# First k stack issued two groups sooner in the key stage, V's maxima begun a group later, the loop's first score moved behind a V group

## The chip, the cores and the metric

The kernel runs on one core of one Trainium2 chip. The metric is the device time of one execution in microseconds (us). Before the change the median of three runs is 1766.57 us (1765.93 to 1769.04).

## The reference

Two attention blocks work on inputs of their own, 2048 positions by 640 columns with 32 heads of 20, and their outputs are joined side by side. Block A attends to a window of 8 positions at a distance of 2. Block B, in which the change lies, is full softmax attention:

```python
qkv = (x @ wqkv).reshape(B, S, 3, H, Dh).transpose(2, 0, 3, 1, 4)
q, k, v = qkv[0], qkv[1], qkv[2]
scores = jnp.einsum("bhqd,bhkd->bhqk", q, k) * (Dh ** -0.5)
p = _softmax(scores, axis=-1)
o = jnp.einsum("bhqk,bhkd->bhqd", p, v)
return o.transpose(0, 2, 1, 3).reshape(B, S, D) @ wo
```

## The kernel before, in words

Each fp32 operand of a projection is split into a high part (an fp32r copy) and a low part (the difference), and three matmuls take the place of one: high by high, high by low, low by high (`PASSES`). PE is TensorE, DVE is VectorE, ACT is ScalarE, POOL is GpSimd; SP is the engine on which nearly all DMAs are issued. Every engine keeps the order in which the code is written.

The stages run one after the other. First the q, k and v of block A are projected. Then come k and q of block B: five pairs of weight tiles (`m` from 0 to 8), each with four blocks of 512 positions (`n`) and two tiles (`j`). A tile is 15 matmuls on PE; ACT casts the result (`pr`), DVE takes the difference, and SP stores both, 512 KB, to `qb_d` or `kb_d` in DRAM. In the last pair, `m == 8`, loads for what follows stand between these stores:

- `wide_pieces(wv_b[0])`, three pieces of the first half of V's weights, into `stg`; ACT casts each into `ww` (high), DVE subtracts (low). In (n, j) = (3, 0) the three pieces of the second half are issued at once, and their casts stand on ACT behind the copy of the second V group.
- `b_keys(0)`, the first group's k stack `bk`: four loads from `kb_d`, of 40, 22, 40 and 22 rows of 16 KB (640 and 352 KB), one each behind the tiles of n = 2 and n = 3.
- `b_queries(0, qc)`, the q rows `bq`: four loads for each of four blocks `qc`, issued behind V's groups.

Then V of block B is projected in 32 groups (`v_group`, L958): 15 matmuls into one bank of PSUM, a copy by ACT into one of four `ve` tiles, a store by SP to `vb_d`. The groups take the position blocks 2, 3, 0, 1, and in each first the four groups of the first weight half, then four of the second. So the fifth group is the first that needs the second half. The last two groups (`v_late`) belong to the loop. From the seventh group on a step of maxima, `b_max` (L753), follows each group: four matmuls of q by k for 128 queries and 1024 keys in two heads, into two pairs of banks (banks 4 to 7, `wide`), and one DVE reduction of each pair. All 24 steps (`LEAD`) must be through before the loop.

The loop (`b_units`, L883) is written out by hand as lists of tokens. `P` adds one step of exponentials by V (the first two `P` are V's two late groups), `ss` is two scores, `MM` two maxima, `sm` one of each, `G` and `V` are work of block A. Each token takes its banks by a planner's clocks (`one`, `two`, L143). The first unit of 16 steps uses `UNIT_V`, as do those that follow it. It begins:

```python
    UNIT_V = (
        "sm P sm MM ss P sm ss MM sm P ss MM sm P sm sm MM sm V sm ss MM sm P sm MM ss P sm MM sm ss P sm MM "
```

Of the kernel before, what the change touches and what calls it, by code (L numbers as in the profile page):

```python
# [40 lines left out]
NKB = 16  # L41
UP = 12
NS = NG * NQC * NKB
LEAD = 24
# [21 lines left out]
def attention_pair(ctx, tc, xa, wqk_a, wv_a, wo_a, xb, wqk_b, wv_b, wo_b, oa, ob):  # L66
# [13 lines left out]
    def after(n, fn, *args):  # L80
        due.setdefault(now[0] + n, []).append((fn, args))
# [22 lines left out]
    def tick():  # L104
        now[0] += 1
        for fn, args in due.pop(now[0], ()):
            fn(*args)
# [81 lines left out]
    def big(home, shape, name):  # L189

        return sb.tile(shape, F32R, tag=f"big{home}", bufs=1, name=name)
# [6 lines left out]
    def chunk(t, xi, k):  # L198
        return t[k // (KC - 1)][:, xi, k % (KC - 1)]

    def x_pieces(x, n, second=None, at=()):

        t = columns(*at or (n,))
        src = x[:, n * 512:(n + 1) * 512].rearrange("(k p) c -> p k c", p=128)

        def piece(a, b):
            u = t[a // (KC - 1)]
            m = a % (KC - 1)
            split(u[:, 0, m:m + b - a], u[:, 1, m:m + b - a], src[:, a:b], "p", second)
        return t, [lambda a=a, b=b: piece(a, b) for a, b in PAIRS]  # L210
# [55 lines left out]
    def m_pieces(m):  # L266
        w = sb.tile([128, 2, KC, 128], F32R, tag="w", bufs=4, name="w")
        return w, [lambda: split(w[:, 0], w[:, 1], wqk_b[m])]
# [35 lines left out]
    NT = S // 128  # L304
# [11 lines left out]
    t, more = x_pieces(xa, 1, at=(2,))  # L316
# [5 lines left out]
    t, loads = x_pieces(xa, 2, at=(3,))  # L322
# [263 lines left out]
    def b_keys(g):  # L586
        k = big(3 * (g % 2), [128, 2, S], "bk")
        v = sb.tile([128, NKB, VG], F32, tag="vb", bufs=2, name="vb")
        stacks[g] = (k, v)
        return [lambda r=r, r0=r0, s0=s0, n=n: sp.dma_start(  # L590
            k[r * HALF + r0:r * HALF + r0 + n].bitcast(F32), kb_d[s0:s0 + n, g * GH + 2 * r:g * GH + 2 * r + 2])
            for r in range(2) for r0, s0, n in BK_RUNS]
# [14 lines left out]
    def dst_b(m, n):  # L607
        def rows(d):
            return d[:2 * DH].rearrange("(t d) h s -> t (d h) s", t=2)[:, (m % KC) * 128:(m % KC + 1) * 128]
        return rows(qb_d[n]) if m < KC else rows(kb_d)[:, :, n * 512:(n + 1) * 512]  # L610

    groups = 0
    for m in range(0, 10, 2):
        nxt = []
        for n in range(4):
            for j in range(2):
                p = next(banks)
                for k in range(KC):
                    for i, (wi, xi) in enumerate(PASSES):
                        pe.matmul(p, WB[j][:, wi, k], chunk(XB[n], xi, k), start=(k == 0 and i == 0),  # L620
                                  stop=(k == KC - 1 and i == 2))
                c = MS[m + j]
                o = (0, 1) if c < KC else (1, 0)
                pt = sb.tile([128, 2, 512], F32R, tag="p", bufs=PB, name="pr")
                act.copy(pt[:, o[0]], p)
                dve.tensor_tensor(pt[:, o[1]], p, pt[:, o[0]].bitcast(F32), ALU.subtract)
                after(1, sp.dma_start, dst_b(c, n).rearrange("t p c -> p t c"), pt.bitcast(F32))
                tick()
                if loads:
                    loads.pop(0)()  # L630
                if m < 8 and (n, j) in ((1, 0), (1, 1)):
                    w, loads = m_pieces(MS[m + 2 + len(nxt)])
                    nxt.append(w)
                elif m == 8 and (n, j) == (0, 1):
                    WV, loads = wide_pieces(wv_b[0])
                elif m == 8 and n == 3:
                    if j == 0:
                        wait[0] = 4
                        w1, more = wide_pieces(wv_b[1])
                        for fn in more:  # L640
                            fn()
                if m == 8 and n > 1:
                    if (n, j) == (2, 0):
                        k_loads = b_keys(0)
                        rings.append(big(1, [128, NQC, 2, 512], "bq"))
                        q_loads = [fn for qc in range(NQC) for fn in b_queries(0, qc)]
                    k_loads.pop(0)()
                groups += 1
                if 4 < groups < 34 and groups * 2 % 5 < 2:
                    next(a_work, None)  # L650
        WB = nxt
# [112 lines left out]
    P = {}  # L764
# [71 lines left out]
    def b_two(what):  # L836
# [35 lines left out]
    PAIR = "P ss MM sm P sm ss MM sm sm".split()  # L872
    UNIT = (
        "P ss MM sm P sm ss MM sm sm P ss MM sm P sm MM ss sm sm P sm MM ss P sm MM ss sm sm P ss MM sm P "
        "sm MM ss sm sm P ss MM sm P sm ss MM ss G sm ss MM sm P sm MM ss P sm MM sm ss P sm MM ss P sm "
        "MM sm ss P MM MM ss P ss MM sm sm").split()
    UNIT_V = (
        "sm P sm MM ss P sm ss MM sm P ss MM sm P sm sm MM sm V sm ss MM sm P sm MM ss P sm MM sm ss P sm MM "
        "ss P sm MM sm ss P sm sm sm P sm ss MM ss G sm MM ss sm P sm MM ss P sm MM sm ss P sm sm sm P sm ss "
        "MM sm P sm MM ss P sm MM ss").split()  # L880
    SLOT = UNIT[:UNIT.index("G")].count("P") - 1

    def b_units(pv, group, more):  # L883

        scores = ((i, pl, r) for i in range(NS - LEAD) for pl in range(2) for r in range(2))
        maxima = ((m, j) for m in range(LEAD, NS) for j in range(2))
        steps = iter(range(-LAG, NS))
        half = []
        for i in range(0, NS - LEAD, NKB):
            for t in UNIT_V if i // NKB < 6 * (NT - UP) else UNIT if i + NKB <= NS - LEAD else PAIR * (NKB // 4):  # L890
                if t == "P":
                    yield
                    pv(next(steps))
                elif t == "G":
                    group()
                elif t == "V":
                    more()
                elif t == "ss":
                    b_two([("s", *next(scores)) for _ in range(2)])
                elif t == "MM":  # L900
                    m, j = next(maxima)
                    max_tiles(m)
                    b_two([("m", m, j, r) for r in range(2)])
                    max_end(m, 1)
                else:
                    s = next(scores)
                    shut = bool(half)
                    m, j, r = half.pop() if shut else (*next(maxima), 1 - s[2])
                    max_tiles(m)
                    if not shut:  # L910
                        half.append((m, j, 1 - r))
                    b_two([("s", *s), ("m", m, j, r)])
                    if shut:
                        max_end(m, 1)
# [39 lines left out]
    steps = iter(range(LEAD))  # L954
    WV = [WV, w1]
    groups = 0
# [66 lines left out]
    for n, half, s in V_GROUPS[:-LAG]:  # L1023
        v_group(n, half, s)
        tick()
        groups += 1
        if q_loads:
            for _ in range(4 if groups == 1 else 1):
                q_loads.pop(0)()
        if groups == 1:  # L1030
            wait[0] = 5
        if groups in (8, 16):
            XB[groups // 8 - 1], more = x_pieces(xb, groups // 8 - 1, gp, (groups // 8 - 1, groups // 8 + 1))
            for fn in more:
                fn()
        if groups > 6:
            for i in islice(steps, 1):
                b_max(i)
        if groups in (9, 11, 15, 17, 19, 23, 25, 28):
            next(a_work, None)  # L1040
        if groups in (22, 23, 26):
            v_piece(0, *((8, 12), (12, 16), (0, 4))[(groups - 21) // 2])
        if groups in (18, 21):
            a_columns(UP + groups // 21)
        if groups == 24:
            for n, fn in enumerate(a_load()):
                after(2 + n, fn)
        if groups == 14:
            a_turn(*done_a.pop(0)[1:])
        turn_parts()  # L1050
        if groups == 28:
            wait[0] = 2
            load_out(wo_a, WO, (0,))
        if loads and groups >= 28:
            loads.pop(0)()
# [33 lines left out]
    steps = b_units(lambda i: b_pv(i) if i >= 0 else v_group(*v_late.pop(0)), group, a_more)  # L1089
    next(steps)  # L1090
    for i in range(NS + LAG):
# [12 lines left out]
        if i > 14 and i % 4 == 3 and next(a_work, 0) == 0:  # L1104
            for d in done_a:
                d[0] -= 1
        if i % NKB == SLOT and done_a and done_a[0][0] <= 0:
            beside.append((lambda d=done_a.pop(0): a_turn(*d[1:]),))
# [76 lines left out]
```

## Time and profile before

| | |
|---|---|
| median of the runs | 1766.57 us (1765.93 to 1769.04) |
| the profiled execution | 1765.34 us |
| its span in the trace | 1763.5 us |
| PE busy | 1749.7 us (99%) |
| DVE / ACT / POOL busy | 1346.4 / 1333.1 / 1229.7 us |
| share of the chain that ended last: PE, DVE | 88%, 6% |
| granted PE clock | 1.00 |
| DMA over the span | 152 GB/s |

The profiled execution's own time is its span and 1.84 us around it. A row of the timeline gives the start in us from the span's start, the time that the row's instructions take together, the engine, the operation with its tiles (written from read), and how many instructions the row joins; in square brackets stands how long the engine was idle before, and what released it. Tiles of PSUM are all called `ps_st`. `ww,xn` and `ww,xl` are a V group, `bk,bq` (read by PE as q by k) a maximum, `bq,bk` a score, `e,vb` a `P`. SPq is SP's queue, in which the issue of a DMA takes some 0.4 us and can wait like any instruction.

### The profile page before, as it was taken

Reading aid. Unit: us, or ns where it says so; the run is one execution under the profiler, and the core shown is the slowest. Engines: PE = TensorE matmul, PEld = TensorE weight load, DVE = VectorE, ACT = ScalarE, POOL = GpSimd, SP = SyncE. Lnnn points to the kernel's source line nnn. Section 1 sums busy time; section 2 is a strip of 40 time slices with the busy share of each in tenths; the row PEclk is TensorE's granted clock in tenths of the full one; section 3 lists DMA queues with packets and bytes.
Section 4 is the critical chain, followed back from the end, with each engine's and each line's share of the span. In section 5 each row is a group of like instructions: output and inputs, shape, how many; then the busy total and the mean of one; then the engine's idle time right before and its main releaser. Section 6 shows DMA issues by size and latency. Waiting matters only on the chain.

```text
span 1763.5 us, 31971 instructions
## 1 busy us (share of the span) xinstructions
PE 1749.7 (99%) x11331; PEld 998.7 (57%) x11331; DVE 1346.4 (76%) x1821; ACT 1333.1 (76%) x2598; POOL 1229.7 (70%) x1086
## 2 busy tenths in 40 slices
PE   9999999999999999999999999999999999999999
PEld 7988888874454444444444444444444444444569
DVE  3102333679999999999999999999999999999400
ACT  4323222229989999999999999989999999989981
POOL 0000683595888888888989888988888888745442
PEclk9999999999999999999999999999999999999999
DMA  7657868774536554644474456536552635222123
GB/s 260 194 172 241 301 240 268 239 233 118 158 100 172 142 163 127 152 134 135 154 172 138 133 150 157 160 100 177 140 159 91 144 109 143 62 73 63 57 72 114
DMA packets 212152, 269.74 MB, mean 153 GB/s; under 512 B 91676, under 2 KB 131740, under 8 KB 211000
## 3 DMA queue, kind: packets, MB, share of 16 engines
q1 hardware_dynamic: 211416, 267.04, 50.5%
q8 instruction: 89, 1.46, 0.3%
q10 hardware_dynamic: 576, 0.66, 0.1%
q14 instruction: 71, 0.58, 0.1%
HBM read 192.87 MB, written 74.74 MB: 152 GB/s over the span
## 4 chain that ended last, share of the span: by engine, by line
PE 88%; DVE 6%; POOL 2%; DMA 1%; issue 1%; ACT 1%; SPq 0%; DVEq 0%; POOLq 0%; ACTq 0%
PE ps_st L61 88%; DVE mx L61 6%; POOL akv L61 1%; DMA bk<-kb_d 1%; ACT e L61 1%; POOL xn L61 0%; DMA vb_d<-ve 0%; SPq L61 0%; POOL ww L61 0%; POOL braw L61 0%; DMA stg<-xa 0%; POOL ao L61 0%; DMA rb<-s_d 0%; POOL xl L61 0%; POOL aot L61 0%
## 5 line engine op out<-in xcount | busy, mean ns | idle before, releaser
L61 DVE TENSOR_REDUCE mx<-ps_st 128x1 f32<-128x512 f32 (+1 forms) x1500 | 1219.3, 879 | 76.0 <-PE ps_st L61 66.2
L61 ACT ACTIVATE e<-ps_st 128x512 f32<-128x512 f32 x2048 | 1067.3, 608 | 36.3 <-PE ps_st L61 17.8
L61 PE MATMUL ps_st<-bq,bk 62*128 62x512 f32 x2048 | 610.3, 440 | 0.8 <-DVE mx L61 0.6
L61 PEld LDWEIGHTS ps_st<-bq,bk 62*128 62x128 f32 x2048 | 288.4, 184 | 479.0 <-ACT e L61 351.9
L61 PE MATMUL ps_st<-bk,bq 60*128 60x512 f32 x2048 | 555.4, 433 | 2.6 <-DVE mx L61 1.8
L61 PE MATMUL ps_st<-e,vb 128*32 128x512 f32 x4096 | 542.9, 604 | 3.2
L61 POOL TENSOR_TENSOR braw<-braw,more 128x512 f32<-128x512 f32 x224 | 287.9, 1285 | 147.3 <-ACT more L61 137.2
L61 POOL TENSOR_TENSOR akv<-akv,aq 128x1280 f32<-128x1280 f32 x64 | 188.5, 2946 | 184.7 <-DMA akv<-ka_d 184.7
L61 POOL TENSOR_TENSOR akv<-akv 128x640 f32<-128x640 f32 (+3 forms) x304 | 282.7, 930 | 23.8
L61 PEld LDWEIGHTS ps_st<-bk,bq 60*128 60x128 f32 x2048 | 269.4, 184 | 34.0 <-DVE mx L61 12.5
L61 ACT COPY ro<-ps_st 128x320 f32<-128x320 f32 (+2 forms) x132 | 62.6, 476 | 192.2 <-PE ps_st L61 160.0
L61 PEld LDWEIGHTS ps_st<-e,vb 128*32 128x32 f32 x4096 | 82.0, 108 | 158.9 <-issue 72.4
L61 POOL TENSOR_TENSOR akv<-akv,al 128x1280 f32<-128x1280 f32 x64 | 151.9, 2374 | 0.2
L61 ACT COPY more<-ps_st 128x512 f32<-128x512 f32 x224 | 132.5, 592 | 1.6 <-PE ps_st L61 1.4
L61 PE MATMUL ps_st<-ww,xn 128*128 128x320 f32 x768 | 125.8, 314 | 0.0
L61 PEld LDWEIGHTS ps_st<-ww,xn 128*128 128x128 f32 x768 | 113.6, 188 | 19.7 <-ACT e L61 8.4
L61 PE MATMUL ps_st<-xn,w 128*128 128x512 f32 x480 | 117.6, 393 | 0.0
L61 PEld LDWEIGHTS ps_st<-xn,w 128*128 128x128 f32 x480 | 90.1, 188 | 21.0
L61 ACT CAST pr<-ps_st 128x512 fp32r<-128x512 f32 x40 | 23.6, 589 | 103.5 <-PE ps_st L61 103.5
L61 PE MATMUL ps_st<-wc,xn 128*128 128x512 f32 (+1 forms) x432 | 101.5, 380 | 0.1
L61 DVE TENSOR_TENSOR pr<-ps_st,pr 128x512 fp32r<-128x512 f32 x40 | 27.7, 692 | 93.0 <-ACT pr L61 90.2
L61 PEld LDWEIGHTS ps_st<-wc,xn 128*128 128x128 f32 x432 | 80.3, 189 | 14.2 <-ACT xn L61 0.5
(71 smaller groups left out, 1065.7 us busy)
## 6 DMA issues: line engine op xcount, KB each, us to landing
akv<-ka_d SPq DMA_DIRECT2D x128, 320.0 KB
akv<-va_d SPq DMA_DIRECT2D x128, 320.0 KB
wx<-wa_d SPq DMA_DIRECT2D x24, 480.0 KB
kb_d<-pr SPq DMA_DIRECT2D x20, 512.0 KB
qb_d<-pr SPq DMA_DIRECT2D x20, 512.0 KB
bk<-kb_d SPq DMA_DIRECT2D x16, 640.0 KB
bq<-qb_d SPq DMA_DIRECT2D x64, 160.0 KB
rb<-s_d SPq DMA_DIRECT2D x128, 64.0 KB
```

Source lines behind the costliest of these rows:

```text
L61: return self.tc.keep_in_program_order(op(*a, **k))
```

## The change

Three edits. In the key stage the four loads of the first k stack stand behind the tiles of n = 1 and n = 2, and two loads of q take their old places behind n = 3; behind the first V group two q loads are issued in place of four, so that all sixteen are through at the same group as before. The maxima begin behind the eighth V group, with two steps behind the twelfth. The first unit of the loop begins with `P` and then `sm`.

```diff
-                if m == 8 and n > 1:
+                if m == 8 and n:
+                    if (n, j) == (1, 0):
+                        first_loads = b_keys(0)
                     if (n, j) == (2, 0):
-                        k_loads = b_keys(0)
                         rings.append(big(1, [128, NQC, 2, 512], "bq"))
                         q_loads = [fn for qc in range(NQC) for fn in b_queries(0, qc)]
-                    k_loads.pop(0)()
+                        first_loads += [q_loads.pop(0) for _ in range(2)]
+                    first_loads.pop(0)()
...
+    UNIT_0 = ["P", "sm"] + UNIT_V[2:]
...
-            for t in UNIT_V if i // NKB < 6 * (NT - UP) else UNIT if i + NKB <= NS - LEAD else PAIR * (NKB // 4):
+            for t in UNIT_0 if not i else UNIT_V if i // NKB < 6 * (NT - UP) else UNIT if i + NKB <= NS - LEAD else PAIR * (NKB // 4):
...
         if q_loads:
-            for _ in range(4 if groups == 1 else 1):
+            for _ in range(2 if groups == 1 else 1):
                 q_loads.pop(0)()
...
-        if groups > 6:
-            for i in islice(steps, 1):
+        if groups > 7:
+            for i in islice(steps, 1 + (groups == 12)):
                 b_max(i)
```

SP's order in the last pair of the key stage, where `qb_d<-pr` is the store of a tile, `stg<-wv_b` a piece of V's weights and `bk<-kb_d` a load of the k stack:

```order
 L61 DMA qb_d<-pr 128x2x512 x2
 L61 DMA stg<-wv_b 128x640
+L61 DMA bk<-kb_d 40x4096
 L61 DMA qb_d<-pr 128x2x512
 L61 DMA stg<-wv_b 128x640
+L61 DMA bk<-kb_d 22x4096
 L61 DMA qb_d<-pr 128x2x512
 L61 DMA stg<-wv_b 128x320
```

The first two loads of the stack now stand between the pieces of the first weight half. A little further down the same engine, from the three pieces of the second half to V's first store (`vb_d<-ve`), with `bq<-qb_d` a load of q:

```order
 L61 DMA stg<-wv_b 128x640 x2
 L61 DMA stg<-wv_b 128x320
-L61 DMA bk<-kb_d 40x4096
+L61 DMA bq<-qb_d 20x1024
 L61 DMA qb_d<-pr 128x2x512
-L61 DMA bk<-kb_d 22x4096
-L61 DMA vb_d<-ve 128x336
-L61 DMA bq<-qb_d 20x1024
-L61 DMA bq<-qb_d 40x1024
+L61 DMA bq<-qb_d 40x1024
+L61 DMA vb_d<-ve 128x336
```

The third and fourth load of the stack are gone from behind the second weight half; they stand ahead of it now, behind the tiles of n = 2. On PE, at V's twelfth group:

```order
 L61 MATMUL ps_st<-ww,xn 128x320 x12
 L61 MATMUL ps_st<-ww,xl 128x320 x3
+L61 MATMUL ps_st<-bk,bq 128x512 x8
+L61 MATMUL ps_st<-ww,xn 128x320 x12
+L61 MATMUL ps_st<-ww,xl 128x320 x3
 L61 MATMUL ps_st<-bk,bq 128x512 x4
 L61 MATMUL ps_st<-ww,xn 128x320 x12
```

Eight matmuls of maxima stand in a row where four did. On PE at the end of V's groups and the start of the loop:

```order
-L61 MATMUL ps_st<-bk,bq 128x512 x4
-L61 MATMUL ps_st<-ww,xn 128x320 x12
-L61 MATMUL ps_st<-ww,xl 128x320 x3
-L61 MATMUL ps_st<-bk,bq 128x512 x4
-L61 MATMUL ps_st<-bq,bk 128x512
-L61 MATMUL ps_st<-bk,bq 128x512
-L61 MATMUL ps_st<-ww,xn 128x320 x12
-L61 MATMUL ps_st<-ww,xl 128x320 x3
+L61 MATMUL ps_st<-bq,bk 128x512
+L61 MATMUL ps_st<-bk,bq 128x512
 L61 MATMUL ps_st<-bq,bk 128x512
 L61 MATMUL ps_st<-bk,bq 128x512 x3
```

The score with its maximum (`bq,bk` and `bk,bq`, one each) stood between the last step of maxima and V's first late group; it now stands behind that group, ahead of the block of six that was there.

## The prediction

> **What bounds the kernel now.** I read the head of the page first, then the chain of waits in order of time, then the timeline of TensorE (PE), VectorE (DVE), ScalarE (ACT) and the DMA issuer (SP) from 285 to 400 us, the only stretch in which the change moves anything.
>
> ```profile
> span 1763.5 us, 31971 instructions
> PE 1749.7 (99%) x11331; PEld 998.7 (57%) x11331; DVE 1346.4 (76%) x1821; ACT 1333.1 (76%) x2598; POOL 1229.7 (70%) x1086
> PE 88%; DVE 6%; POOL 2%; DMA 1%; issue 1%; ACT 1%; SPq 0%; DVEq 0%; POOLq 0%; ACTq 0%
> ```
>
> PE is busy 99% of the span and carries 88% of the chain. So the time changes by what PE gains or loses between the V groups and the loop's first units, and I follow PE's program there.
>
> ```profile
> 309.99 1.92 PE L61 MATMUL ps_st<-ww,xn 128*128 128x320 f32 x12
> ...
> 314.39 1.92 PE L61 MATMUL ps_st<-ww,xn 128*128 128x320 f32 x12
> 316.15 0.60 PE L61 MATMUL ps_st<-ww,xl 128*128 128x320 f32 x3
> 316.68 0.50 PE L61 MATMUL ps_st<-bk,bq 60*128 60x512 f32 x1
> 317.59 0.70 PE L61 MATMUL ps_st<-bk,bq 60*128 60x512 f32 x3 [0.41 <-DMA vb_d<-ve]
> 318.22 2.02 PE L61 MATMUL ps_st<-ww,xn 128*128 128x320 f32 x12
> ...
> 320.62 0.73 PE L61 MATMUL ps_st<-bk,bq 60*128 60x512 f32 x4
> 321.28 2.03 PE L61 MATMUL ps_st<-ww,xn 128*128 128x320 f32 x12
> ```
>
> A row of 12 with its row of 3 is one V group of 15 matmuls; a row of 4 is one step of maxima. Two V groups without maxima take 314.39 - 309.99 = 4.40 us, 2.20 each. A V group behind a step takes 320.62 - 318.22 = 2.40, and a step 321.28 - 320.62 = 0.66. The first step, behind the seventh group, is the exception: one matmul goes, the next three wait, and it takes 318.22 - 316.68 = 1.54.
>
> **The change, part by part.**
>
> (a) The first step moves behind the eighth group, 2.20 us later for PE than now. The operands that it waits for are in by 317.59, and the new place is at 316.68 + 2.20 = 318.88, so the wait goes even if nothing lands sooner: 1.54 - 0.66 = **0.88 us saved**. (What else the loads do is part e.)
>
> (b) 24 steps now stand behind 23 groups. One V group is no longer behind a step: 2.40 - 2.20 = **0.20 saved**.
>
> (c) Behind the twelfth group stand two steps. A step uses both pairs of banks, so the second must wait for DVE to read the first. No such doubling is in the trace; the nearest rows are those where DVE is late for another reason:
>
> ```profile
> 321.17 2.36 DVE L61 TENSOR_REDUCE mx<-ps_st 128x2 f32<-128x1024 f32 x2 [0.71 <-PE ps_st L61]
> ...
> 368.61 2.34 DVE L61 TENSOR_REDUCE mx<-ps_st 128x2 f32<-128x1024 f32 x2
> ...
> 369.87 0.49 PE L61 MATMUL ps_st<-bk,bq 60*128 60x512 f32 x2 [0.28 <-DVE mx L61]
> 371.00 0.50 PE L61 MATMUL ps_st<-bk,bq 60*128 60x512 f32 x2 [0.64 <-DVE mx L61]
> 371.44 2.03 PE L61 MATMUL ps_st<-ww,xn 128*128 128x320 f32 x12
> ```
>
> DVE starts 321.17 - 320.62 = 0.55 after a step's first matmul. A pair is free 369.87 - 368.61 = 1.26 after its reduction starts, the next pair 1.13 later, and the V group follows 0.44 after that. Two steps in a row thus take 0.55 + 1.26 + 1.13 + 0.44 = 3.38 instead of 2 x 0.66 = 1.32: **2.06 lost**. The bounds are 0 and 2 x 2.36 - 1.32 = 3.4; I take 2.06, since it is built from rows of the same instruction. DVE's backlog is gone by the next step: it rests 0.71 us in front of each, and the next V group gives it 2.4 us. The waits at 369.87 and 371.00 stand behind the same groups after the change and stay.
>
> (d) The loop's first score with its maximum goes from the end of the last step to behind V's first late group.
>
> ```profile
> 389.10 0.73 PE L61 MATMUL ps_st<-bk,bq 60*128 60x512 f32 x4
> 389.67 0.39 PE L61 MATMUL ps_st<-bq,bk 62*128 62x512 f32 x1
> 390.92 0.49 PE L61 MATMUL ps_st<-bk,bq 60*128 60x512 f32 x1 [0.86 <-DVE mx L61]
> 391.35 2.02 PE L61 MATMUL ps_st<-ww,xn 128*128 128x320 f32 x12
> ...
> 393.74 0.73 PE L61 MATMUL ps_st<-bk,bq 60*128 60x512 f32 x3
> 394.30 0.55 PE L61 MATMUL ps_st<-bq,bk 62*128 62x512 f32 x2
> 394.79 2.02 PE L61 MATMUL ps_st<-ww,xn 128*128 128x320 f32 x12
> ```
>
> The maximum waits for the bank that DVE still reads. From 389.10 to the V group are 2.25 us instead of 0.66, so removing the pair saves 1.59. In its new place DVE is through, since the V group gives it 2.4 us. The pair joins a block of six matmuls that takes 394.79 - 393.74 = 1.05; two more cost half a step, 0.33, or nothing, where that block already waits for ACT's copy of the V group. I take 0.15: **1.44 saved** (1.26 to 1.59). Four exponentials instead of three then stand behind one V copy on ACT, with a V group of cover behind them.
>
> (e) Two loads of the k stack (640 and 352 KB) move past three loads of V's second weight half in SP's queue. How much that matters I read from what SP waits for.
>
> ```profile
> SPq L61 <- DMA bk<-kb_d: 6.5, 3, 4.0
> ...
> SPq L61 <- DMA stg<-wv_b: 1.4, 3, 0.5
> ```
>
> ```profile
> 303.15 0.42 SPq L61 DMA_DIRECT2D bk<-kb_d  x1
> 304.43 0.33 SPq L61 DMA_DIRECT2D vb_d<-ve  x1
> 305.57 0.29 SPq L61 DMA_DIRECT2D bq<-qb_d  x1
> 306.28 0.29 SPq L61 DMA_DIRECT2D bq<-qb_d  x1
> 307.08 0.27 SPq L61 DMA_DIRECT2D bq<-qb_d  x1
> 307.82 0.27 SPq L61 DMA_DIRECT2D bq<-qb_d  x1
> 312.15 0.34 SPq L61 DMA_DIRECT2D vb_d<-ve  x1
> ...
> 315.40 0.34 SPq L61 DMA_DIRECT2D vb_d<-ve  x1
> ```
>
> From 285 to 325 us SP waits three times for k loads, 4.0 us at most (in front of 312.15), and three times for weight loads. The issue that waits for a transfer stands eight places behind it in SP's order: eight transfers are in flight. Counted back by eight, these issues mark landings: second k load 304.43, a store of q 305.57, the three weight loads 306.28, 307.08 and 307.82, third k load 312.15, fourth 315.40. The third k load therefore took 312.15 - 307.82 = 4.33, the fourth with a store of q 3.25, less the store's 305.57 - 304.43 = 1.14: 2.11. Together 6.4 us, now ahead of the weights. Against that stands the queue's idle time while the first loads go out:
>
> ```profile
> 286.00:294.00 8.00, 8.00 (x36) 6.45 (x36) 2.14 (x3) 1.80 (x3) 0.00 (x0) 1.00 0.76 255
> 308.00:312.00 4.00, 4.00 (x29) 4.00 (x28) 1.08 (x2) 1.04 (x3) 0.00 (x0) 1.00 0.60 173
> ```
>
> The last two columns are the DMA engines' busy share and GB/s. From 308 to 312 us, with little but k and q loads in flight, 0.60 of 16 engines are busy at 173 GB/s: 9.6 engines at 18 GB/s each. From 286 to 294 us 24% is idle, 1.9 us. So the weights land 6.4 - 1.9 = 4.5 us later, the first piece at 310.8. Who needs it:
>
> ```profile
> 306.29 2.00 ACT L61 CAST ww<-stg 128x640 fp32r<-128x640 f32 x3
> ...
> 307.05 2.03 DVE L61 TENSOR_TENSOR ww<-stg,ww 128x640 fp32r<-128x640 f32 x3 [4.34 <-ACT ww L61]
> ```
>
> ACT starts its cast in the moment of the landing (306.28), and DVE's first difference, some 0.8 of the 2.03, ends at 307.9. The fifth V group, at 309.99, takes that half in its third matmul, two matmuls of 2.20 / 15 later, at 310.3. The slack is 2.4 us, the delay 4.5: **2.1 lost**. From below it is bounded by nothing (no wait if the delay is under 2.4), from above by 6.4 - 2.4 = 4.0, if none of the idle time is used. The cover that goes is this slack: PE has four banks of V's copies in hand, but no other work. The first half's last piece (issued before the third k load) has the first and second in front of it and 1.3 us or more to spare, so I cost it at nothing. The first q loads come later behind the backlog, by my sum about 317, before the first step at 318.88 + 2.1.
>
> [...]
>
> **The sum**: -0.88 - 0.20 + 2.06 - 1.44 + 2.1 = +1.64. The profiled execution took 1765.34 us (span 1763.5 and 1.84 around it), so 1766.98; it lay 1.23 below the median of the runs, 1766.57, which becomes **1768.2**. Behind the loop's first two V groups each engine's order is as before, so I carry the shift to the end unchanged.
>
> **Rivals.** *The loads fit in* (1766.1): part (e) is nothing and the rest is -0.46. For it: the idle share may be used better than I count, and a delay under 2.4 us costs nothing; against it: 4.33 us for one load in the trace, and a cast that starts in the moment of the landing. [...] *The loads choke the queue* (1770.8, slower beyond what a measurement tells): beside the stores of q the four loads run slower still. If 6.4 us become 9, the delay is 7.1 and the wait before the fifth group 4.7, 2.6 more. It decides from about 13 GB/s an engine in place of 18. Against it: 304.43 for the second load leaves the first two little more than the last two took. *The double is hidden* (1766.1): (c) costs nothing, if the reductions free the banks earlier; the rows at 369.87 and 371.00 speak against it. *The first step waits anyway* (1769.1): the q loads, behind the backlog, land after the eighth group, and (a)'s 0.88 stays, so the change doesn't do what it says; they would have to be 4 us later than I work out.
>
> **How the numbers follow.** A measurement of this kernel tells some 0.2%, 3.5 us, from no change. Forecast 50%, loads fit in 26%, choke 13%, double hidden 6%, first step waits 5%. The 1766.1 cases reach down to 1765.2 with the runs' scatter (their lowest lies 0.64 below the median); above, (c) and (e) at 3.4 and 2.8 give 1770.2. So 1765.2 to 1770.2 leaves out most of the choke and little else. Faster by over 0.2% needs 1763.0, both lost terms gone and more: 3%. Slower needs 1770.1: the choke and the forecast's upper end, 13%. Same 84%.
>
> **What would show it.** PE's timeline: a gap inside or before the fifth V group (4.3 us to the sixth instead of 2.2), none before the first step, 3.4 us for the row of eight with a wait on DVE, none of 0.86 at the loop's start. SP: issues held up from 302 to 312. ACT: the weight casts near 310.8 instead of 306.29. I am wrong if the fifth group starts on time, or if PE's rows differ behind the loop's first two V groups by anything but a shift.

## The result and the profile after

The changed kernel takes 1769.22 us (median of 22 runs, 1766.94 to 1773.0) where the kernel before takes 1766.03 (22 runs): a ratio of 1.0016, 95% interval 1.0009 to 1.0022. The interval lies above 1, so this is a loss, but the ratio is under the 0.2% that I had set as the bound of "same". The forecast was 1768.2, and its range to 1770.2 holds the median. The median itself rose by 3.19 us, where the sum had +1.64.

The profiled execution of the changed kernel took 1766.94 us, 1.60 more than the one of before; the sum had been +1.64. It was the fastest of the 22 runs. So two things need an answer: whether each term of the sum is where I put it, and why the median of the runs lies another 1.6 us higher than the profile explains. First the head of the page, the shares of the chain, and what PE waits for (total us, times, longest):

```profile
span 1765.2 us, 31968 instructions
PE 1749.8 (99%) x11331; PEld 999.0 (57%) x11331; DVE 1346.1 (76%) x1821; ACT 1333.1 (76%) x2598; POOL 1230.5 (70%) x1086
PE 93%; DVE 4%; ACT 1%; issue 1%; DMA 1%; POOL 0%; DVEq 0%; SPq 0%; POOLq 0%; ACTq 0%
```

```profile
PE ps_st L61 <- DVE mx L61: 3.3, 5, 1.1
PE ps_st L61 <- POOL ident L61: 1.4, 1, 1.4
PE ps_st L61 <- ACT ww L61: 1.0, 1, 1.0
PE ps_st L61 <- DVE ww L61: 0.3, 1, 0.3
```

PE works as long as before (1749.8 against 1749.7) and carries 93% of the chain, so the added 1.7 us of span are waits. Two of these rows are new: PE waits for ACT and then DVE to prepare V's weights (`ww`). The timeline of PE shows where, and what became of the other places:

```profile
307.71 1.92 PE L61 MATMUL ps_st<-ww,xn 128*128 128x320 f32 x12
...
311.10 0.56 PE L61 MATMUL ps_st<-ww,xn 128*128 128x320 f32 x2 [1.03 <-ACT ww L61]
311.96 1.74 PE L61 MATMUL ps_st<-ww,xn 128*128 128x320 f32 x10 [0.30 <-DVE ww L61]
...
313.98 1.92 PE L61 MATMUL ps_st<-ww,xn 128*128 128x320 f32 x12
...
320.67 0.74 PE L61 MATMUL ps_st<-bk,bq 60*128 60x512 f32 x4
321.34 2.03 PE L61 MATMUL ps_st<-ww,xn 128*128 128x320 f32 x12
...
332.91 0.74 PE L61 MATMUL ps_st<-bk,bq 60*128 60x512 f32 x4
334.73 0.50 PE L61 MATMUL ps_st<-bk,bq 60*128 60x512 f32 x2 [1.09 <-DVE mx L61]
335.86 0.50 PE L61 MATMUL ps_st<-bk,bq 60*128 60x512 f32 x2 [0.63 <-DVE mx L61]
336.30 2.03 PE L61 MATMUL ps_st<-ww,xn 128*128 128x320 f32 x12
...
391.88 0.73 PE L61 MATMUL ps_st<-bk,bq 60*128 60x512 f32 x4
392.54 2.02 PE L61 MATMUL ps_st<-ww,xn 128*128 128x320 f32 x12
...
394.93 0.50 PE L61 MATMUL ps_st<-bq,bk 62*128 62x512 f32 x1
...
396.18 2.03 PE L61 MATMUL ps_st<-ww,xn 128*128 128x320 f32 x12
```

From the top: behind the fourth V group at 307.71, the fifth waits 1.03 and then 0.30 us; the first step of maxima does not wait (321.34 - 320.67 = 0.67); the double step takes 336.30 - 332.91 = 3.39; at the loop's start the last step takes 0.66 to the late group, and the block that received the moved score takes 396.18 - 394.93 = 1.25, where the smaller block took 1.05.

ACT's rows tell when the second weight half came: its casts start in the moment in which the load lands (here the chain of waits has the landing at 310.30 and the cast at 310.32), and that moved from 306.29 to 310.32.

```profile
310.32 1.91 ACT L61 CAST ww<-stg 128x640 fp32r<-128x640 f32 x3 [4.19 <-DMA stg<-wv_b]
```

The stretch in which I had counted on idle DMA engines is fuller indeed, 0.94 of them busy where it was 0.76 (the last two columns: share and GB/s):

```profile
286.00:294.00 8.00, 8.00 (x36) 6.49 (x35) 2.14 (x3) 1.80 (x3) 0.00 (x0) 1.00 0.94 267
```

**What the profile doesn't explain.** Each run also records its mean granted PE clock. Of the changed kernel's 22 runs, the 7 at 1.000 average 1767.49 us; 10 at 0.999 average 1769.47, 4 at 0.998 average 1771.22, one at 0.997 took 1772.11. The profile above is one of the 7. Over all the comparisons below, the kernel before was at 1.000 in 74 of 96 runs, which average 1765.79. (One more execution of it, at a clock of 0.753 and 2024.6 us, is left out of these counts and means.) At full clock the change thus costs 1767.49 - 1765.79 = 1.7 us, as the trace has it. The rest of the median's distance goes with the granted clock: a thousandth of it is 1.77 us over the span, and the averages rise by 1.98 from 1.000 to 0.999 and by 1.75 from there to 0.998.

### The profile page after: what moved, and what is told of

Read it like the earlier page. It is cut to its first block, busy times and chain, and to the rows that moved or that the text cites. A ratio compares the mean times of both kernels' runs of the same rounds, so it can differ in the third digit from the quotient of the medians.

```text
span 1765.2 us, 31968 instructions
## 1 busy us (share of the span) xinstructions
PE 1749.8 (99%) x11331; PEld 999.0 (57%) x11331; DVE 1346.1 (76%) x1821; ACT 1333.1 (76%) x2598; POOL 1230.5 (70%) x1086
## 4 chain that ended last, share of the span: by engine, by line
PE 93%; DVE 4%; ACT 1%; issue 1%; DMA 1%; POOL 0%; DVEq 0%; SPq 0%; POOLq 0%; ACTq 0%
PE ps_st L61 93%; DVE mx L61 4%; ACT e L61 1%; DMA stg<-wv_b 1%; DVE mtr L61 0%; POOL am L61 0%; ACT more L61 0%; DVE ww L61 0%; ACT ww L61 0%; DVE xl L61 0%; DVE pr L61 0%; ACT al L61 0%; ACT pr L61 0%; DVEq L61 0%; ACT xl L61 0%
```

## The experiments

**Two theories for the remaining 1.6 us.** *The clock theory*: the change gives PE two new places of rest, before the fifth V group (1.33 us in two pieces) and in the double step (1.72 us in two), and in some runs the granted clock falls behind them for a while. Such a stretch is called a dip here. *The landing theory*: in the slower runs the weights land later still, so that the wait itself is longer. By the first, a kernel with one of the two rests has dips at that place, and work on PE in place of the rest takes them away. By the second, all of it goes with the loads, and work in the rests changes nothing.

The results together; "below 1.000" counts the runs whose mean granted clock is under that, and the last column is the mean of the others:

| kernel | median us (range), runs | ratio to before (95%) | below 1.000 | mean at 1.000 |
|---|---|---|---|---|
| before, in three comparisons | 1766.42, 1765.79, 1765.77 | | 12 of 34, 2 of 33, 8 of 29 | 1765.93, 1765.92, 1765.47 |
| changed | 1769.22 (1766.94–1773.0), 22 | 1.0016 (1.0009–1.0022) | 15 of 22 | 1767.49 |
| loads only | 1769.24 (1766.79–1772.26), 12 | 1.0014 (1.0006–1.0023) | 9 of 12 | 1768.49 |
| maxima only | 1768.02 (1766.18–1773.3), 11 | 1.0006 (0.9997–1.0015) | 10 of 11 | 1766.18 (one run) |
| score only | 1765.3 (1764.09–1771.63), 12 | 0.9994 (0.9986–1.0003) | 3 of 12 | 1765.22 |
| changed, loads undone | 1767.13 (1765.12–1771.24), 12 | 0.9999 (0.999–1.0008) | 7 of 12 | 1765.33 |
| three loads sooner, score | 1763.98 (1762.97–1767.6), 11 | 0.999 (0.9981–0.9999) | 1 of 11 | 1763.93 |
| changed, three loads sooner | 1767.19 (1766.19–1768.08), 11 | 1.0006 (0.9997–1.0015) | 8 of 11 | 1767.00 |
| loads undone, double filled | 1765.71 (1764.86–1767.22), 11 | 1.0001 (0.9992–1.001) | 5 of 11 | 1765.24 |
| changed, both filled (8) | 1768.06 (1767.41–1770.82), 11 | 1.0015 (1.0006–1.0024) | 4 of 11 | 1767.89 |
| changed, both filled (16) | 1767.49 (1766.72–1774.95), 12 | 1.0013 (1.0004–1.0021) | 4 of 12 | 1767.64 |
| three loads sooner alone | 1764.79 (1763.71–1768.79), 11 | 0.9998 (0.999–1.0007) | 4 of 11 | 1764.82 |
| changed, again | 1769.26 (1768.6–1770.83), 11 | 1.0021 (1.0012–1.003) | 11 of 11 | none |

Loads only to loads undone were compared on one chip, the next four kernels on a second, the last three on a third. The kernel before itself is below 1.000 in 35%, 6% and 28% of its runs on these three, so counts below 1.000 can only be compared on one chip. Single profiles differ by up to 0.9 us in when the fourth V group begins, so a shift read from one profile carries that much.

**Loads only.** The kernel before with the sooner loads; maxima and score as they were.

```diff
-                if m == 8 and n > 1:
+                if m == 8 and n:
+                    if (n, j) == (1, 0):
+                        first_loads = b_keys(0)
...
+                        first_loads += [q_loads.pop(0) for _ in range(2)]
+                    first_loads.pop(0)()
...
-            for _ in range(4 if groups == 1 else 1):
+            for _ in range(2 if groups == 1 else 1):
```

> The kernel before with the early loads alone: maxima from the seventh group, one step each, the loop's first unit as before. Both theories have the terms of the trace: the fifth V group waits 1.9 us for the second weight half, the first step of maxima no longer waits (0.9 saved), so +1.0 us in a trace at full clock. Theory 1 (what the median of the changed kernel has beyond its trace, about 1.6 us, is granted clock lost around a rest of PE): if the fifth group's rest is the one that costs it, the clock is below 1.000 in most runs and the median stands 2 to 3 us above before; if the double is, the clock stays 1.000 and the median is +1.0. Theory 2 (the rest is the weights landing later still in most runs): median +2 to +3, with the clock at 1.000 in the runs that are longer.

It is as slow as the whole change. Its profile, at a mean clock of 0.999, shows the wait for the weights, somewhat longer (1.95 and 0.30), and something that the profile of the changed kernel does not have:

```profile
311.52 0.56 PE L61 MATMUL ps_st<-ww,xn 128*128 128x320 f32 x2 [1.95 <-ACT ww L61]
312.38 2.76 PE L61 MATMUL ps_st<-ww,xn 128*128 128x320 f32 x10 [0.30 <-DVE ww L61]
```

Ten matmuls take 2.76 us where the changed kernel's took 1.74. The windows of one us there (the third number from the end is the granted clock):

```profile
312.00:313.00 1.00, 0.70 (x4) 0.62 (x4) 1.00 (x2) 0.91 (x3) 0.00 (x0) 0.87 0.82 304
313.00:314.00 1.00, 1.00 (x6) 1.00 (x5) 0.53 (x2) 0.47 (x2) 0.00 (x0) 0.50 0.59 210
...
315.00:316.00 1.00, 1.00 (x5) 1.00 (x5) 0.00 (x0) 0.00 (x0) 0.00 (x0) 0.50 0.75 274
316.00:317.00 1.00, 1.00 (x8) 1.00 (x8) 0.00 (x0) 0.43 (x1) 0.00 (x0) 0.93 0.54 182
```

Right behind PE's rest the clock is 0.50 for about 0.26 + 3 + 0.14 = 3.4 us, which I estimate to cost half of that, 1.7. Both theories find something here: a longer wait and a dip. The clock does not cover everything: of the three runs at 1.000 two lie 0.9 and 1.7 us above the mean of the kernel before at 1.000, around the 1.0 of the rows, and one lies 5.1 above.

**Maxima only.** The kernel before with the later start and the double.

```diff
-        if groups > 6:
-            for i in islice(steps, 1):
+        if groups > 7:
+            for i in islice(steps, 1 + (groups == 12)):
```

> The kernel before with the maxima alone (from the eighth group, two steps behind the twelfth); loads and loop as before. Terms of the trace: no wait of the first step (-0.9), one V group less behind a step (-0.2), the double (+2.1): +1.0 us. Theory 1: clock below 1.000 in many runs and 1 to 2 us more if the double's rest is the one that costs the clock. Theory 2: +1.0 and no more, since no load is moved.

No load moves here, and yet 10 of 11 runs are below 1.000. The V group behind the double step takes 3.44 us in place of 2.03, at half clock from 334.6 to 338.0:

```profile
334.00 0.50 PE L61 MATMUL ps_st<-bk,bq 60*128 60x512 f32 x2 [0.62 <-DVE mx L61]
334.43 3.44 PE L61 MATMUL ps_st<-ww,xn 128*128 128x320 f32 x12
```

That can't come from weights that land late. This profile has a second dip in the loop, near 1417 us, behind two rests of 1.16 and 0.64 us on DVE, and ends 7.98 us behind the profile of before, where the part's own price was 1 us. The kernel with the loads undone rests 1.84 and 0.49 us at the same place and has a dip there too; the profiles of before and of the change do not. Both of these dips last 6.8 us (by the same estimate 3.4 lost). What holds DVE up is in its own row, here of the kernel with the loads undone:

```profile
1412.77 0.25 DVE L61 RECIPROCAL sm<-sm 128x16 f32<-128x16 f32 x1 [4.12 <-DMA sm<-s_d]
```

DVE waits for a small load (tile `sm`, read back from `s_d` in DRAM), and the reductions that free PE's banks stand behind it (here they start at 1413.27). The wait is 3.45 us in this kernel's profile, 1.94 with the loads only (where PE then rests and no dip follows, yet some 1.0 us is lost) and 1.00 with the score only. All four are the profiles of the first chip; in the others it is 0.39 at most. So runs also differ by a load that is no part of the change; why it lands late is open.

**Score only.**

```diff
+    UNIT_0 = ["P", "sm"] + UNIT_V[2:]
...
-            for t in UNIT_V if i // NKB < 6 * (NT - UP) else UNIT if i + NKB <= NS - LEAD else PAIR * (NKB // 4):
+            for t in UNIT_0 if not i else UNIT_V if i // NKB < 6 * (NT - UP) else UNIT if i + NKB <= NS - LEAD else PAIR * (NKB // 4):
```

> The kernel before with the loop's first score behind V's first late group alone. Both theories: -1.4 us (the trace's -1.6 and +0.2), clock as in the kernel before. A rival on this term: the loop gives the 1.4 us back later, then no difference.

At full clock it gains 1765.93 - 1765.22 = 0.71, half of what the score saves at its place: in its profile the loop's first `P` comes 1.30 us sooner than before, but the lead is 0.62 by 889 us and 0.21 at the end. Not all of the 1.30 is the score's: 0.39 is there before V begins (its first group starts at 300.80, in the kernel before at 301.19), and the first step of maxima, which waits longer in this profile, gives 0.53 back. Every kernel here that has the moved score loses 0.2 to 1.1 us in this slow way through the loop; in those without it the shift stays within some 0.2 up to the wait near 1415. That the planner then chooses other banks in some places of the loop would be a reason; this I did not test.

**The change with its loads undone** (maxima and score alone; the diff is the two above together).

> The changed kernel with the loads of before: only the fifth group's wait should go. Terms of the trace: -0.4 us against before, 1.9 below the changed kernel's trace. Theory 1, if the double costs the clock: about +1 with the clock below 1.000 in many runs; if the fifth group's rest does: -0.4 and the clock as before. Theory 2: -0.4.

The sum without (e) was -0.46; at full clock it measures 1765.33 - 1765.93 = -0.60. Yet its median gains nothing, with 7 of 12 runs below 1.000. Its profile has the dip near 1415 and none at the double, though PE rests there as in the changed kernel (1.09 and 0.63).

**Three loads sooner, with the score.** Of the four loads of the k stack the last one goes behind the second weight half; maxima as before, no double.

```diff
-                if m == 8 and n > 1:
+                if m == 8 and n and (n, j) != (2, 1):
+                    if (n, j) == (1, 0):
+                        first_loads = b_keys(0)
...
+                        first_loads.append(q_loads.pop(0))
+                    first_loads.pop(0)()
...
-            for _ in range(4 if groups == 1 else 1):
+            for _ in range(3 if groups == 1 else 1):
```

> The kernel before with three of the four k loads sooner (the fourth behind V's second weight half) and the loop's first score behind V's late group; the maxima start behind the seventh group, one step each. Landings by the sum of the prediction: one load less ahead of the weights, 4.33 + 2 x 2.1 instead of 2 x 6.4 in all, so the first weight piece comes 2.4 us later than before, the edge of the slack: no wait, or a few tenths. The q loads are in at about 316, when the first step comes. So 0.9 saved at the first step and, as the run with the score alone has it at its end, 0.2 to 1.0 by the score: -1 to -2 us. Theory 1 (clock lost around rests of PE): no rest is added and one or two go, so the clock is below 1.000 in no more runs than before, about a third. If the delay comes with the number of bytes moved and not with the two loads ahead of the weights, the fifth group waits over 1 us here too.

This beats both kernels: 1763.98 us, 1.8 below the kernel before on its chip, with one run of 11 below full clock. PE in its profile:

```profile
309.65 2.58 PE L61 MATMUL ps_st<-ww,xn 128*128 128x320 f32 x12
...
317.00 0.73 PE L61 MATMUL ps_st<-bk,bq 60*128 60x512 f32 x4
317.67 2.03 PE L61 MATMUL ps_st<-ww,xn 128*128 128x320 f32 x12
```

The fifth group loses 2.58 - 1.92 = 0.66 in small pieces, and the first step, back behind the seventh group, does not wait (0.67): with sooner loads the first step needs no later place.

**The change with three loads sooner.** Of the change only the fourth load is put back.

```diff
-                if m == 8 and n:
+                if m == 8 and n and (n, j) != (2, 1):
...
-                        first_loads += [q_loads.pop(0) for _ in range(2)]
+                        first_loads.append(q_loads.pop(0))
```

> The changed kernel with three of the four k loads sooner in place of four. If the two loads ahead of V's second weight half are what the fifth group waits for, one of them less (2.1 us) takes the 1.9 us away: 1.5 to 1.9 below the changed kernel in a trace at full clock, like the kernel with the loads of before (-0.4). The double stays, so theory 1 has the clock below 1.000 in about half of the runs, median 0 to +1. If the wait hangs on the first two loads too, a wait of about 1 us stays before the fifth group.

The fifth group starts on time and at full speed, so the wait is the loads ahead of the weights, and one of them decides: ACT's cast starts at 308.51 here (308.49 in the kernel above, with the same loads of k sooner) and at 310.32 in the changed kernel. The clock dips behind the double instead:

```profile
309.68 0.60 PE L61 MATMUL ps_st<-ww,xl 128*128 128x320 f32 x3
310.11 1.92 PE L61 MATMUL ps_st<-ww,xn 128*128 128x320 f32 x12
...
334.63 3.29 PE L61 MATMUL ps_st<-ww,xn 128*128 128x320 f32 x12
```

With 8 of 11 runs below 1.000 the median is 1767.19, though no weights land late. The kernel above differs from this one in the maxima alone and was below in 1 of 11 on the same chip, and the dip here stands behind the double. That kernel's median is 3.2 us lower, where the rows price the maxima at 1.0. Its three runs at 1.000 average 1767.00, only 0.2 below the other eight; why those are not faster the clock theory does not tell.

**Filling the double.** The kernel with the loads undone, and identity transposes on PE in the double's two rests, five and two. Their result is used by nothing.

```diff
+    def keep(n):
+        t = bank()
+        for _ in range(n):
+            pe.transpose(t[:, :128], ident, ident)
+        give(t)
...
+            if n:
+                keep((n, n // 2)[j])
...
+            for n, i in enumerate(islice(steps, 1 + (groups == 12))):
+                b_max(i, 5 * n)
```

> The changed kernel with the loads of before, and PE busy in the double: five transposes of the identity ahead of the second step's first pair and two ahead of its second pair, into a bank that nobody reads, where PE rested 1.1 and 0.6 us. Theory 1 (a rest of PE costs granted clock in some runs): the trace is the same within 0.3 us, but the clock is below 1.000 in about a third of the runs as before, and the median falls to -0.4. Rival (the clock falls with the kernel's mix of work, or by chance): as without the transposes, below 1.000 in 7 of 12, +0.7.

The double takes the time that it took (334.55 - 331.16 = 3.39), since PE's two waits in it still end with DVE, but PE rests only 0.39 and 0.27 us in it, and the V group behind it runs at full speed, 2.03 us:

```profile
331.16 0.73 PE L61 MATMUL ps_st<-bk,bq 60*128 60x512 f32 x4
331.83 0.77 PE L61 MATMUL ps_st<-ident 128*128 128x128 f32 x5
332.99 0.50 PE L61 MATMUL ps_st<-bk,bq 60*128 60x512 f32 x2 [0.39 <-DVE mx L61]
...
334.55 2.03 PE L61 MATMUL ps_st<-ww,xn 128*128 128x320 f32 x12
```

The median falls by 1.4 us against the unfilled kernel, though on another chip, and is level with the kernel before, where I had expected 0.4 less. The share below 1.000 is no support for the clock theory: 5 of 11, where I had expected it as before, which is 2 of 33 on this chip. The dip in this profile stands at 1650, where PE waits 1.4 us for ACT: none at the filled place, one elsewhere.

**Filling both.** The changed kernel, with the double filled in the same way and eight transposes before the fifth V group (`if groups == 4: keep(8)` ahead of `v_group`).

> The changed kernel with PE busy in both rests: eight transposes ahead of the fifth V group, and the seven in the double. The waits themselves stay. Theory 1: the trace stays at +1.6 (up to 0.5 more, where the transposes end after the landing), the clock is below 1.000 in about a third of the runs, and the median falls from +3.2 to +1.6 to +2.1. Rival: clock below 1.000 in two thirds of the runs, +3.2.

A miss at the first place: the eight end near 310.7, the weights came later than usual in this profile (the fifth group starts at 312.82, in the changed kernel's at 311.10), and PE still rested 2.10 us, with a dip behind it. At the double there was none. The share below 1.000, 4 of 11, is what I had expected, but the median, 2.3 us above before, did not come down to the 1.6 to 2.1. So I doubled the number, and ran the changed kernel itself beside it:

```diff
+        if groups == 4:
+            keep(16)
```

> The changed kernel with 16 identity transposes before the fifth V group (about 2.05 us by the 1.03 us that eight took) and five and two inside the double, so PE rests little at either place. The result of the transposes is used by nothing. Clock theory (rests of PE behind the fourth V group and in the double let the granted clock fall): PE's remaining rest before the fifth group is under 1 us when the weights land as in the changed kernel's profile (310.3), the clock stays at 1.00 at 310 to 320 us and at 334 to 340 us, fewer than a third of the runs lie below 1.000, and the median comes down from the changed kernel's 1769.2 to about 1767.7, though work was added. Rival (the runs above 1767.5 come from weights that land later still): as many runs stay slow, median 1769 or above, since transposes bring no weights.

> The changed kernel once more, unaltered, on the same chip as the kernel with both places filled, so that the shares of runs below full clock are compared on one chip. Clock theory: more than half of its runs below 1.000, those at 1.000 near 1767.5, the median near 1769. Rival (the earlier share was a matter of the chip): few runs below 1.000, median near 1767.5 as in the filled kernel.

On one chip the changed kernel was below 1.000 in 11 of 11 runs and took 1769.26; with 23 transposes more it was below in 4 of 12 (a third, where I had said fewer, and near the 8 of 29 of the kernel before) and took 1767.49. Added work that nothing uses made it 1.8 us faster. PE in the filled kernel, from the transposes to the sixth group, and its clock in two windows of 5 us:

```profile
309.18 1.91 PE L61 MATMUL ps_st<-ident 128*128 128x128 f32 x16
311.03 0.56 PE L61 MATMUL ps_st<-ww,xn 128*128 128x320 f32 x2
311.89 1.15 PE L61 MATMUL ps_st<-ww,xn 128*128 128x320 f32 x6 [0.30 <-DVE ww L61]
313.32 0.86 PE L61 MATMUL ps_st<-ww,xn 128*128 128x320 f32 x4 [0.28 <-DVE ww L61]
...
314.46 1.92 PE L61 MATMUL ps_st<-ww,xn 128*128 128x320 f32 x12
```

```profile
310.00:315.00 5.00, 4.43 (x29) 3.73 (x28) 2.05 (x3) 2.47 (x5) 0.00 (x0) 1.00 0.67 230
...
335.00:340.00 5.00, 4.52 (x26) 3.25 (x27) 3.85 (x5) 0.68 (x2) 0.00 (x0) 1.00 0.35 119
```

The sixth group starts at 314.46, later than the changed kernel's 313.98: the wait for the weights is still there, only filled. And the changed kernel's second profile, at a mean clock of 0.998, has the dip behind the double:

```profile
336.27 0.50 PE L61 MATMUL ps_st<-bk,bq 60*128 60x512 f32 x2 [0.63 <-DVE mx L61]
336.70 2.85 PE L61 MATMUL ps_st<-ww,xn 128*128 128x320 f32 x12
```

```profile
337.00:338.00 1.00, 1.00 (x7) 1.00 (x6) 1.00 (x2) 0.00 (x0) 0.00 (x0) 0.80 0.28 105
338.00:339.00 1.00, 1.00 (x5) 1.00 (x5) 0.48 (x1) 0.00 (x0) 0.00 (x0) 0.50 0.00 0
...
340.00:341.00 1.00, 1.00 (x6) 0.50 (x4) 0.00 (x0) 0.57 (x2) 0.00 (x0) 0.50 0.00 0
341.00:342.00 1.00, 1.00 (x9) 0.74 (x6) 0.89 (x1) 1.00 (x2) 0.12 (x1) 0.99 0.29 107
```

Again 0.4 + 3 = 3.4 us at half clock, in the program whose first profile ran through the same rests at full clock. This second profile has one more dip of 3.4 us, near 1652, behind a rest of 0.64 us:

```profile
1650.96 2.12 PE L61 MATMUL ps_st<-bq,bk 62*128 62x512 f32 x8 [0.64 <-DVE mx L61]
```

Every other profile rests here too, the kernel before for 0.63 us, and none but the one with 1.4 us dips here. So a new rest is not needed for a dip, and the kernel before, below 1.000 in 22 of its 96 runs, may have them too.

The clock theory stands in the main, by two comparisons on one chip (1 of 11 runs to 8 of 11 when the double is added, 11 of 11 to 4 of 12 when both places are filled) and by dips behind either rest, in kernels that have only that one too. At the unfilled double three of five profiles dip, at the filled one none of three. The landing theory explains a part as well: the two pieces of the wait before the fifth group are 1.33 and 1.91 us together in the changed kernel's two profiles, 2.25 with the loads only, and 2.40 with eight transposes ahead of them, so the landing varies by 1 to 2 us.

**Three loads sooner, alone.** The kernel with three sooner loads, without the moved score (the diff is that one without `UNIT_0`).

> The kernel before with three of the four k loads sooner, and nothing else: the first step of maxima stays behind the seventh V group, the score stays. If the first step's wait (0.88 us) goes by the loads and the score's place is worth what the kernel with both showed beyond that (1.9 together), this one saves 0.9, less up to 0.66 for a wait inside the fifth V group: about 1765.3 where the kernel before has 1765.9. Rival: the gain of the kernel with both was the score alone, and this one is at nothing or above: 1766 or more.

At full clock it gains 1765.47 - 1764.82 = 0.65, its median 1.0; the ratio's interval includes no change. Neither the fifth group nor the first step waits in its profile. With the score added, the gain at full clock is 1765.92 - 1763.93 = 2.0, so the score is worth about 1.3 there, more than it was alone.

## Why the prediction was right, and what it lacked

- **(a) First step of maxima**: right. It takes 0.67 us at its new place, and there is no wait, as forecast; with the maxima alone, loads as before, there is none either. "The first step waits anyway" falls. What the forecast did not see: with the sooner loads it would not have waited at its old place either (0.67 behind the seventh group in the kernel with three sooner, and no such wait with the loads only), so the later start bought no more than the 0.20 of (b), and the double that it forced cost ten times that.
- **(b) One V group less behind a step**: nothing in the rows speaks against the 0.20; it was too small to be tested by itself.
- **(c) The double**: right, 3.39 us where 3.38 was worked out from the two waits at 369.87 and 371.00. DVE's backlog was gone by the next step, as forecast. "The double is hidden" falls.
- **(d) The score**: right at its place. The step fell from 2.25 to 0.66, the block grew by 0.20 where I took 0.15: 1.39 saved against 1.44. But the score alone brought only 0.71 at full clock.
- **(e) The weights**: mechanism right, size slightly over. Without a wait the sixth V group would start two groups behind the fourth's 307.71, at 312.11; it starts at 313.98, 1.87 later where I had 2.1. The weights landed at about 310.3, by ACT's cast, against my 310.8. Taking one of the two loads back removed the wait in two profiles, and all but 0.66 us of it in a third. "The loads fit in" falls: the landing moved by 310.32 - 306.29 = 4.0 us, past the slack of 2.4, where the 18 GB/s an engine of the trace gave 4.5. "The loads choke the queue" falls too.
- **The sum**: +1.64 forecast, +1.60 in the profiled execution, +1.7 between the runs at full clock.
- **What failed** is the last step, "Behind the loop's first two V groups each engine's order is as before, so I carry the shift to the end unchanged". In the profile this was nearly so: the shift is 1.38 us at the loop's first `P` and 1.61 at the end. In the runs it was not: I carried the shift of an execution at full clock to a median that then contained few of them. The missing step is a question to every new rest of PE, whether the clock holds behind it. It is worth 1769.22 - 1767.49 = 1.7 us, as much as the whole sum. That the median is off by 1.0 only is partly luck: the shift is 3.19 where I had 1.64, and the three runs that I started from had a median 0.54 above that of the 22. The range held because it was wide for other reasons.

## What to carry to other kernels

Work out a moved wait from the nearest rows of the same instruction: the double from two old waits came out within 0.01 us. Two loads moved ahead in SP's queue made the weights behind them land 4.0 us later here (306.29 to 310.32, with the DMA engines 0.94 busy from 286 to 294 us where it had been 0.76), so look for the load behind with the least slack; the best kernel moves three of the four loads and the score and leaves the maxima alone, 1.8 us under the start. And where an engine busy 99% of the span gets new rests, here of 1.33 and 1.72 us, compare the granted clock of the runs (below 1.000 in 11 of 11 here, and in 4 of 12 with both rests filled), on one chip, and not the profile alone: the profile can be one of the few runs in which it held.

## What the hardware showed

- PE's clock was granted at 0.50 for 3.4 us (worked out from the windows of two profiles above: 0.26 + 3 + 0.14 with the loads only, 0.4 + 3 in the changed kernel's second) behind rests of PE of 1.7 to 2.4 us in two pieces, in some runs of a program and not in others: the changed kernel's first profile has rests of 1.33 and 1.72 us and a clock of 1.00 behind both. Single rests of 0.64 and 1.4 us near 1650 were followed by the same 3.4 us, and near 1415 two profiles had twice the length, 6.8 us, behind 1.16 and 0.64 us and behind 1.84 and 0.49. From what rest on the clock falls, and what sets the length, no run here shows.
- Behind a double filled with identity transposes the clock stayed up in all three profiles that have it, and with both places filled 4 of 12 runs were below 1.000 against 11 of 11. Why some runs dip and others, with the same rests, do not was not settled.
- A small load in the loop, `sm<-s_d`, kept DVE waiting 1.0 to 4.1 us near 1410 in the four profiles of one chip and 0.39 at most in all others. Why is open.
